# POOL instead of ACT scales the upper words of fifteen raw output weights

## The chip, the cores and the metric

The kernel runs on one core of one Trainium2 chip. The metric is the device time of one execution in microseconds (us), the median of several. A core has five engines, each with an instruction stream of its own that runs in order: TensorE (PE, whose weight loads are listed as PEld), VectorE (DVE), ScalarE (ACT), GpSimd (POOL) and SyncE (SP, which here issues all DMAs). [...]

## The reference

A windowed attention with 8 heads over 4 sequences of 768 positions, then a feed-forward block with a squared ReLU on the 3072 rows of 512 values:

```python
scores_l = scale * np.matmul(q, k.transpose(0, 1, 3, 2))          # kept where |i - j| < 16
scores_s = scale * np.einsum('bhsd,bhnd->bhsn', q, k_sum) + np.log(block)
a = softmax(concatenate([scores_l_masked, scores_s], axis=-1))
x = np.matmul(a, np.concatenate([v, v_sum], axis=2))               # to [3072, 512]
h = x @ w_in                                                       # [3072, 2048]
r = np.maximum(h, 0.0)
g = s * (r * r) + b
return (g @ w_out).astype(np.float32)
```

`k_sum` is the maximum and `v_sum` the mean over blocks of 32 positions. The weights `w_in` and `w_out` arrive as 64-bit floats.

## The kernel before

The 3072 rows are cut into 12 chunks `c` of 256 rows. For each chunk the attention is computed in four head pairs `p`, and the feed-forward block in 16 hidden blocks `f` of 128: `hidden` (PE, L403) makes the block, `activate` squares it, `project` (PE, L442) adds it to the chunk's output. Chunk 0 multiplies in plain 32-bit floats; later chunks use each operand split in a high and a low part.

The weights of a block are two tiles, ("in", f) and ("out", f), of 128x512 numbers of 64 bits. They come by DMA as they are, 512 KB each (`load_weights`, L111), into tiles named `wraw`, and are made 32-bit floats on the chip. `scale_weights` works in place on the raw words: L118 multiplies the upper word, read as a 32-bit float, by 2^-112, and L119 multiplies the lower word by 2^-29 and writes it as an integer. Both were on ACT. `convert_weights` on DVE then puts the parts together: L132 shifts the scaled upper word and masks it, L134 adds the sign bit to it, L136 adds the lower word; the result is `wf_in_f` or `wf_out_f`. From block 2 on, in and out are converted together, each of the three steps for in and then for out. Block f of chunk 0 needs `wf_in_f` in `hidden` and `wf_out_f` in `project`; in chunk 1 `split_weights` (L145 on ACT, L147 on DVE) makes the parts for later chunks.

All 32 tiles are thus converted while chunk 0 runs, from about 18 to 87 us, beside the attention of chunks 0 and 1: maximum and mask on DVE (L314), exponentials on ACT (L327), normalization on DVE (L337), copies of results on ACT (L353, L384) and the low part of the attention's output on DVE (L386). POOL builds masks in the first 8 us, then has nothing until it copies block maxima behind the window's keys (L250) for chunk 2 at 69 us. From chunk 1 on it computes `g` (L423) and fills values (L255).

The order of everything is written out by hand: the string `FIRST_ORDER` for the start (A is `scale_weights`, B `convert_weights`, H `hidden`, J `activate`, P `project`), and a plan of steps after it, one step for each hidden block. Scaling of block f stands at step f - 3 and conversion at step f - 2. Nothing is rescheduled after that, so each engine runs its instructions in the order in which the code issues them. The tiles `wraw` share 16 slots with other tiles, and SP's queue loads into a slot when its last user is done.

Of the kernel before, what the change touches and what calls it, by code (L numbers as in the profile page):

```python
# [14 lines left out]
AF = mybir.ActivationFunctionType  # L15
ALU = mybir.AluOpType
# [28 lines left out]
def windowed_attention_then_relu2_ffn(ctx, tc, qk, vwin, kt, vt, kq, vrow, wp, sb, out):  # L45


    nc = tc.nc
# [49 lines left out]
    for base, sign in ((0, 1), (BLOCK - 1, -1)):  # L98
        nc.gpsimd.affine_select(
            out=mean4[:, KR - 4 : KR], in_=mean4[:, KR - 4 : KR], compare_op=ALU.is_ge, fill=0.0,  # L100
# [12 lines left out]
    def scale_weights(key):  # L113


        raw = w_raw[key]
        top = raw[:, :, 1].bitcast(F32)
        nc.scalar.activation(top, top, AF.Copy, scale=2.0**-112)  # L118
        nc.scalar.activation(raw[:, :, 0].bitcast(I32), raw[:, :, 0], AF.Copy, scale=2.0**-29)  # L119

    def convert_weights(*keys):
# [351 lines left out]
    for n, name in enumerate(FIRST_ORDER.split()):  # L473
        kind, i = name[0], int(name[1:])
        if kind in loads:
            at(FIRST + 1, n, loads[kind], i)
        elif kind == "R":
            at(FIRST + 1, n, *((mean_of_rows, i) if i < 3 else (mean_done,)))
        elif kind == "A":
            at(FIRST + 1, n, scale_weights, ("in" if i % 2 == 0 else "out", i // 2))  # L480
        elif kind == "W":
            at(FIRST + 1, n, keep_warm, i)
        elif kind == "Z":
            at(FIRST + 1, n, scores_of_maxima, i)
        elif kind in steps:
            at(FIRST + 1, n, steps[kind], 0, i)
            ahead.add((kind, i))
        elif kind == "B":
            at(FIRST + 1, n, convert_weights, ("in" if i % 2 == 0 else "out", i // 2))
        elif kind == "D":  # L490
            at(FIRST + 1, n, convert_weights, ("in", i), ("out", i))
        elif kind in halves:
            for j in range(2):
                at(FIRST + 1, n, halves[kind], 0, i, j)
        else:
            at(FIRST + 1, n, stages[kind], 0, i)
# [42 lines left out]
    for f in range(NF):  # L539
        for side in ("in", "out"):  # L540
            if f >= 6:
                at(f - 9, LOAD, load_weights, (side, f))
            if 2 * f + (side == "out") >= FIRST_SCALED:
                at(f - 3, WEIGHTS, scale_weights, (side, f))
        if f >= FIRST_TURNED:
            at(f - 2, WEIGHTS, convert_weights, ("in", f), ("out", f))
        for side in ("in", "out"):
            at(NF - 3 + f, SPLIT, split_weights, (side, f))
# [72 lines left out]
```

## Time and profile before

| | |
|---|---|
| median of 3 runs | 641.46 us (639.6 to 641.55) |
| profiled execution, first to last instruction | 639.9 us |
| mean granted TensorE clock | 0.999 of full speed |
| ACT L118, upper words | 32 of 128x512, median 672 ns |
| ACT L119, lower words | 32 of 128x512, median 676 ns |
| DVE L132, L134, L136 for one tile | medians 418, 682 and 680 ns |
| POOL L423, 128x256 | 176, mean 623 ns |
| POOL between 8 and 64 us | no instruction |

Of the profiled execution only its span is listed; the runs' times include what lies ahead of the first instruction and behind the last. In the views, each row of a timeline gives the start and the length in us, the engine, the line, the operation and its tiles (written, then read), and in brackets how long the engine was idle before it and what released it. [...]

### The profile page before, as it was taken

Reading aid. Unit: us, or ns where it says so; the run is one execution under the profiler, and the core shown is the slowest. Engines: PE = TensorE matmul, PEld = TensorE weight load, DVE = VectorE, ACT = ScalarE, POOL = GpSimd, SP = SyncE. Lnnn points to the kernel's source line nnn. Section 1 sums busy time; section 2 is a strip of 40 time slices with the busy share of each in tenths; the row PEclk is TensorE's granted clock in tenths of the full one; section 3 lists DMA queues with packets and bytes.
Section 4 is the critical chain, followed back from the end, with each engine's and each line's share of the span. In section 5 each row is a group of like instructions: output and inputs, shape, how many; then the busy total and the mean of one; then the engine's idle time right before and its main releaser. Section 6 shows DMA issues by size and latency. Waiting matters only on the chain.

```text
span 639.9 us, 14293 instructions
## 1 busy us (share of the span) xinstructions
PE 631.2 (99%) x5316; PEld 553.3 (86%) x5316; DVE 329.4 (51%) x1081; ACT 327.7 (51%) x982; POOL 165.1 (26%) x325
## 2 busy tenths in 40 slices
PE   9899999999999999999999999999999999999997
PEld 7566678889999999999998998998999899899896
DVE  5997988885436335436526235345624514512311
ACT  3999988845437436426346345346336336423321
POOL 3000004143142421331251151151141232232211
PEclk9999999999999999999999999999999999999999
DMA  9999406035102211600700400700530400200000
GB/s 330 385 387 362 133 1 188 2 103 192 49 2 83 96 39 54 203 14 30 214 22 2 166 28 11 256 1 14 142 109 14 165 2 14 71 2 1 34 1 34
DMA packets 25606, 63.27 MB, mean 99 GB/s; under 512 B 3968, under 2 KB 3968, under 8 KB 25536
## 3 DMA queue, kind: packets, MB, share of 16 engines
q1 hardware_dynamic: 25536, 62.36, 29.1%
q8 instruction: 42, 0.69, 0.4%
q14 instruction: 28, 0.23, 0.1%
HBM read 55.90 MB, written 6.29 MB: 97 GB/s over the span
## 4 chain that ended last, share of the span: by engine, by line
PE 91%; ACT 6%; DVE 2%; issue 0%; DVEq 0%
PE po L442 40%; PE ph L403 39%; PE pav L374 3%; PE pt L346 3%; PE ps L293 3%; ACT wraw L118 2%; ACT wraw L119 2%; PE warm L202 1%; ACT pr L327 1%; ACT r L413 1%; PE pm L210 0%; PE ps L297 0%; ACT g L419 0%; ACT r L412 0%; DVE wf_in L136 0%
## 5 line engine op out<-in xcount | busy, mean ns | idle before, releaser
L423 POOL TENSOR_SCALAR g<-r,sb_col 128x256 f32<-128x256 f32 x176 | 109.5, 623 | 386.6 <-ACT r L413 282.2
L412 ACT ACTIVATE r<-ph 128x256 f32<-128x256 f32 x192 | 72.5, 378 | 214.9 <-PE ph L403 201.4
L425 DVE CAST gh<-g 128x256 fp32r<-128x256 f32 x176 | 53.3, 303 | 249.4 <-POOL g L423 241.9
L442 PE MATMUL po<-wh,gl 128*128 128x512 f32 x352 | 141.1, 401 | 0.0
L442 PE MATMUL po<-wh,gh 128*128 128x512 f32 x352 | 138.5, 393 | 0.0
L442 PE MATMUL po<-wl_out,gh 128*128 128x512 f32 x352 | 137.4, 390 | 0.0
L403 PE MATMUL ph<-xh,wl_in 128*128 128x256 f32 x704 | 110.2, 279 | 0.0
L403 PE MATMUL ph<-xl,wh 128*128 128x256 f32 x704 | 108.6, 276 | 0.0
L403 PE MATMUL ph<-xh,wh 128*128 128x256 f32 x704 | 108.6, 276 | 0.0
L403 PEld LDWEIGHTS ph<-xh,wl_in 128*128 128x128 f32 x704 | 97.2, 188 | 5.2 <-ACT r L413 0.5
L427 DVE TENSOR_TENSOR gl<-g,gh 128x256 fp32r<-128x256 f32 x176 | 81.0, 460 | 30.5 <-PE po L442 13.9
L403 PEld LDWEIGHTS ph<-xl,wh 128*128 128x128 f32 x704 | 93.4, 188 | 0.0
L403 PEld LDWEIGHTS ph<-xh,wh 128*128 128x128 f32 x704 | 92.9, 188 | 0.0
L413 ACT ACTIVATE r<-r 128x256 f32<-128x256 f32 x192 | 80.3, 418 | 6.1
L327 ACT ACTIVATE pr<-pr,mn 128x120 f32<-128x120 f32 x176 | 67.0, 382 | 32.0 <-DVE mn L314 31.9
L442 PEld LDWEIGHTS po<-wh,gh 128*128 128x128 f32 x352 | 66.1, 188 | 14.4
L442 PEld LDWEIGHTS po<-wh,gl 128*128 128x128 f32 x352 | 66.2, 188 | 13.9 <-issue 1.6
L442 PEld LDWEIGHTS po<-wl_out,gh 128*128 128x128 f32 x352 | 66.2, 188 | 13.0
L255 POOL COPY vw<-vsum 24x256 f32<-24x256 f32 x80 | 38.6, 513 | 10.6 <-PE po L442 4.5
L403 PEld LDWEIGHTS ph<-x,wf_in 128*128 128x128 f32 x128 | 23.6, 190 | 12.4 <-issue 2.9
L450 ACT COPY o<-po 128x512 f32<-128x512 f32 x24 | 14.1, 587 | 38.8 <-PE po L442 36.2
L403 PE MATMUL ph<-x,wf_in 128*128 128x256 f32 x128 | 31.1, 385 | 2.2 <-ACT pr L327 1.3
(82 smaller groups left out, 636.8 us busy)
## 6 DMA issues: line engine op xcount, KB each, us to landing
wraw<-in_wp_dram SPq DMA_DIRECT2D x32, 512.0 KB
qk<-in_qk_dram SPq DMA_DIRECT2D x44, 368.0 KB
vw<-in_vwin_dram SPq DMA_DIRECT2D x48, 192.0 KB
out_dram<-o SPq DMA_DIRECT2D x24, 256.0 KB
kraw<-in_kt_dram SPq DMA_DIRECT2D x12, 384.0 KB
vraw<-in_vt_dram SPq DMA_DIRECT2D x12, 252.0 KB
kq<-in_kq_dram SPq DMA_DIRECT2D x4, 512.0 KB
vraw<-in_vt_dram SPq DMA_DIRECT2D x6, 264.0 KB
```

Source lines behind the costliest of these rows:

```text
L255: filler(c).tensor_copy(vw_t[c, p][WIN:KR, e], vsum[bi][WIN : WIN + NB, 2 * p + e, :].unsqueeze(1).to_broadcast([NB, NSUB, D]),)
L293: nc.tensor.matmul(o, qi, kw[r, i, :], start=True, stop=True)
L327: nc.scalar.activation(pr, pr, AF.Exp, bias=mn_of[c, p][:, n : n + 1], scale=-1.0, accum_out=sm_of[c, p][:, n : n + 1])
L346: nc.tensor.transpose(pt_of[c, p][:KR, n * P : (n + 1) * P], pr[:, n, :], ident)
L374: nc.tensor.matmul(oi, vw[:, e, i, :], pi, start=True, stop=True)
L403: nc.tensor.matmul(ph, w[:, kc * P : (kc + 1) * P], x[:, kc], start=(n == 0), stop=(n == len(terms) - 1))
L412: nc.scalar.activation(r, ph, AF.Relu)
L413: nc.scalar.activation(r, r, AF.Square)
L423: nc.gpsimd.tensor_scalar(g, r, s_col, b_col, ALU.mult, ALU.add)
L425: nc.vector.tensor_copy(gh, g)
L427: nc.vector.tensor_tensor(gl, g, gh.bitcast(F32), ALU.subtract)
L442: nc.tensor.matmul(po[t], a[:, t * P : (t + 1) * P], w, start=(f == 0 and n == 0), stop=(f == NF - 1 and n == len(terms) - 1),)
```

## The change

In `scale_weights` the upper words of the output weights of blocks 1 to 15 are multiplied by POOL. The output weights of block 0, all 16 tiles of input weights, and all lower words stay on ACT.

```diff
         raw = w_raw[key]
         top = raw[:, :, 1].bitcast(F32)
-        nc.scalar.activation(top, top, AF.Copy, scale=2.0**-112)
+        if key[0] == "out" and key[1] > 0:
+            nc.gpsimd.tensor_scalar(top, top, 2.0**-112, None, ALU.mult)
+        else:
+            nc.scalar.activation(top, top, AF.Copy, scale=2.0**-112)
         nc.scalar.activation(raw[:, :, 0].bitcast(I32), raw[:, :, 0], AF.Copy, scale=2.0**-29)
```

Three lines are added, so that L119 of before is L122 after it, L132 is L135, and so on.

ACT's queue before, from the g of block 1 on (`wraw_323` and `wraw_346` are the in and out tiles of block 3, then follow those of blocks 4 and 5):

```order
L419 ACTIVATE g0_481<-r_478,sb_col_89 128x256
L118 ACTIVATE wraw_323<-wraw_323 128x512
L119 ACTIVATE wraw_323<-wraw_323 128x512
L118 ACTIVATE wraw_346<-wraw_346 128x512
L119 ACTIVATE wraw_346<-wraw_346 128x512
L118 ACTIVATE wraw_377<-wraw_377 128x512
L119 ACTIVATE wraw_377<-wraw_377 128x512
L118 ACTIVATE wraw_379<-wraw_379 128x512
L119 ACTIVATE wraw_379<-wraw_379 128x512
```

And the same place after the change:

```order
L422 ACTIVATE g0_481<-r_478,sb_col_89 128x256
L121 ACTIVATE wraw_323<-wraw_323 128x512
L122 ACTIVATE wraw_323<-wraw_323 128x512
L122 ACTIVATE wraw_346<-wraw_346 128x512
L121 ACTIVATE wraw_377<-wraw_377 128x512
L122 ACTIVATE wraw_377<-wraw_377 128x512
L122 ACTIVATE wraw_379<-wraw_379 128x512
```

One of the four ACT instructions of each block is gone; the rest keep their order. POOL's queue after the change, at the last five of the moved instructions (output weights of blocks 11 to 15), with the first fills of keys behind them:

```order
L119 TENSOR_SCALAR wraw_555<-wraw_555 128x512
L119 TENSOR_SCALAR wraw_592<-wraw_592 128x512
L119 TENSOR_SCALAR wraw_640<-wraw_640 128x512
L119 TENSOR_SCALAR wraw_681<-wraw_681 128x512
L119 TENSOR_SCALAR wraw_736<-wraw_736 128x512
L253 COPY qk_827<-ksum_164 128x4x24
L253 COPY qk_829<-ksum_190 128x4x24
```

Before, those fills came right behind the masks; now all fifteen stand between, with nothing of another kind among them. In DVE's queue nothing moves; what changes is for whom it waits. Before, at the conversion of block 3:

```order
L132 TENSOR_SCALAR wf_in_3_521<-wraw_323 128x512 [waits DMAHW3_49,Activation_49]
L132 TENSOR_SCALAR wf_out_3_522<-wraw_346 128x512 [waits DMAHW4_49,Activation_49]
L134 SCALAR_TENSOR_TENSOR wf_in_3_521<-wraw_323,wf_in_3_521 128x512 [waits DVE_49]
L134 SCALAR_TENSOR_TENSOR wf_out_3_522<-wraw_346,wf_out_3_522 128x512 [waits DVE_49]
L136 ISA wf_in_3_521<-wraw_323,wf_in_3_521 128x1024 [waits DVE_49]
L136 ISA wf_out_3_522<-wraw_346,wf_out_3_522 128x1024 [waits DVE_49,Activation_49]
```

After it:

```order
L135 TENSOR_SCALAR wf_in_3_521<-wraw_323 128x512 [waits DMAHW3_49,Activation_49]
L135 TENSOR_SCALAR wf_out_3_522<-wraw_346 128x512 [waits DMAHW4_49,Pool_49]
L137 SCALAR_TENSOR_TENSOR wf_in_3_521<-wraw_323,wf_in_3_521 128x512 [waits DVE_49]
L137 SCALAR_TENSOR_TENSOR wf_out_3_522<-wraw_346,wf_out_3_522 128x512 [waits DVE_49]
L139 ISA wf_in_3_521<-wraw_323,wf_in_3_521 128x1024 [waits DVE_49,Activation_49]
L139 ISA wf_out_3_522<-wraw_346,wf_out_3_522 128x1024 [waits DVE_49,Activation_49]
```

The first step for the out tile waits for POOL instead of ACT.

## The prediction

> **What bounds the kernel now.** The page comes first: its span, the busy shares, and the shares of the chain that ended last.
>
> ```profile
> span 639.9 us, 14293 instructions
> PE 631.2 (99%) x5316; PEld 553.3 (86%) x5316; DVE 329.4 (51%) x1081; ACT 327.7 (51%) x982; POOL 165.1 (26%) x325
> PE 91%; ACT 6%; DVE 2%; issue 0%; DVEq 0%
> ```
>
> The matrix engine PE carries 91% of the chain; ACT carries 6%, about 38 us. Averages hide where those lie, so the second view is the table of busy time by stretch:
>
> ```profile
> core 0: us, PE busy (x) PEld busy (x) DVE busy (x) ACT busy (x) POOL busy (x), PEclk, DMA share, GB/s
> 40.00:48.00 8.00, 8.00 (x59) 5.16 (x58) 7.93 (x25) 7.87 (x19) 0.00 (x0) 1.00 1.03 365
> 56.00:64.00 8.00, 8.00 (x83) 5.46 (x82) 4.71 (x12) 7.90 (x22) 0.00 (x0) 1.00 1.03 358
> ```
>
> While the first chunk runs and weights are converted (about 24 to 90 us), ACT **and** DVE are both full; POOL is empty. DVE has room in one stretch only. Third view, DVE's waits between 24 and 92 us (total, times, longest):
>
> ```profile
> DVE xl L386 <- ACT xh L384: 3.2, 1, 3.2
> DVE wf_out L132 <- ACT wraw L118: 0.5, 1, 0.5
> ```
>
> That is all DVE lost there, 3.68 us with the 3.22 and 0.46 that the timeline gives for them. So DVE is nearly as much the limit as ACT. Fourth view, the chain in order of time (start, length):
>
> ```profile
> 59.49 0.56 ACT wraw L118
> 62.24 0.42 DVE xl L386
> 69.74 0.68 DVE wf_in L136
> 70.55 1.97 PE ph L403 x8
> ```
>
> Up to 62 us the chain runs on ACT, from 62.24 to 70.4 on DVE, and from 70.55 it stays on PE until the end of the first chunk, and nearly without a break until the program ends. So what the change does to the time is what it does to the matmul that starts at 70.55 (hidden block 11): if that is late by x, the end is late by x. After it, PE waits for nothing that conversion delivers; the last block's weights are there 2.25 us ahead (85.54 + 0.68, against 88.47):
>
> ```profile
> 85.54 0.68 DVE L136 CUSTOM_DVE_ANT_0 wf_in<-wraw,wf_in 128x1024 uint16<-128x1024 uint16 x1
> 88.47 1.89 PE L403 MATMUL ph<-x,wf_in 128*128 128x256 f32 x8
> ```
>
> Where PE stood before 70.55 says how much could be won:
>
> ```profile
> 39.26 1.10 PE L403 MATMUL ph<-x,wf_in 128*128 128x256 f32 x4 [1.26 <-ACT pr L327]
> 51.69 0.70 PE L403 MATMUL ph<-x,wf_in 128*128 128x256 f32 x2 [0.27 <-ACT r L412]
> 70.55 0.67 PE L403 MATMUL ph<-x,wf_in 128*128 128x256 f32 x2 [0.47 <-DVE wf_in L136]
> 38.44 0.68 DVE L136 CUSTOM_DVE_ANT_0 wf_in<-wraw,wf_in 128x1024 uint16<-128x1024 uint16 x1
> ```
>
> The first wait is put down to ACT, but the weights of that block came from DVE at 38.44 + 0.68 = 39.12: it is DVE's. Of the three, counted from the usual spacing of such groups, some 1.3, 0.4 and 0.6 us are lost.
>
> **The change part by part.** *Removed from ACT:* 15 of these 32 instructions, at the chain's step of 0.57 us (0.67 each, the next starting earlier):
>
> ```profile
> L118 ACT ACTIVATE wraw<-wraw x32: 650/672/710, 18.1 to 79.6; 128x512 f32<-128x512 f32 x32
> ```
>
> 15 × 0.57 = 8.6 us of ACT time. Little of it can reach the end: DVE does all of its work still. DVE's 3.68 us of idle time can go, no more. And PE can at best be earlier by 0.46 at block 4 (DVE's wait at 33 us), 0.4 at block 7 (ACT's) and 0.6 at block 11: 1.5 us is the ceiling.
>
> *Added to POOL:* 15 TENSOR_SCALARs of 128x512, in POOL's queue ahead of the first fill of window keys (L250). Each waits for its DMA, not for ACT's turn, so it runs when its weights land. The last loads go out in this row (SP's queue) and ACT scales the last one 24 us later, from data that had long landed:
>
> ```profile
> 51.92 3.82 SPq L111 DMA_DIRECT2D wraw<-in_wp_dram  x4
> 79.62 0.68 ACT L118 ACTIVATE wraw<-wraw 128x512 f32<-128x512 f32 x1
> ```
>
> So all 15 run between about 20 and 66 us, several us ahead of need. POOL's own length is thus hidden: even at 1.5 us each, with one due every 3 to 4 us, nothing waits for it. The fills of keys behind them started at 69.25 and come after the last of the 15 in any case.
>
> *What is not hidden is the memory port.* POOL and DVE get in each other's way here. The timeline, POOL alone, then with DVE:
>
> ```profile
> 95.31 0.56 POOL L423 TENSOR_SCALAR g<-r,sb_col 128x256 f32<-128x256 f32 x1 [24.18 <-ACT r L413]
> 504.98 0.59 POOL L423 TENSOR_SCALAR g<-r,sb_col 128x256 f32<-128x256 f32 x1 [0.17 <-POOL g L423]
> 505.25 0.60 DVE L427 TENSOR_TENSOR gl<-g,gh 128x256 fp32r<-128x256 f32 x1
> 506.15 0.43 DVE L427 TENSOR_TENSOR gl<-g,gh 128x256 fp32r<-128x256 f32 x1
> ```
>
> The subtraction takes 0.43 alone and 0.60 when POOL began 0.27 earlier: it was held until 0.27 + 0.17 = 0.44 after POOL's start. The same, the other way round, among the very conversions at issue:
>
> ```profile
> 133.41 0.26 POOL L250 COPY qk<-ksum 128x96 f32<-128x96 f32 x1 [0.56 <-issue]
> 324.29 0.40 POOL L255 COPY vw<-vsum 24x256 f32<-24x256 f32 x1 [0.44 <-PE po L442]
> 69.06 0.68 DVE L134 SCALAR_TENSOR_TENSOR wf_out<-wraw,wf_out 128x512 uint32<-128x512 uint32 x1
> 69.25 0.61 POOL L250 COPY qk<-ksum 128x96 f32<-128x96 f32 x1 [61.58 <-DVE wf_in L134]
> 69.66 0.75 DVE L136 CUSTOM_DVE_ANT_0 wf_in<-wraw,wf_in 128x1024 uint16<-128x1024 uint16 x1
> ```
>
> A copy that takes 0.26 alone (0.40 at 256 elements) takes 0.61 under L134: it waits for the running DVE instruction, then gets in before the next one, which takes 0.75 instead of 0.68. So **POOL's wait is free, but each POOL operation pushes DVE back** by what it streams.
>
> How much? The copy pushed DVE by 0.07, so 0.19 of its 0.26 lies off the port. Taking 0.19 from L423's 0.56 leaves 0.37 for 256 elements, thus 0.74 for 512. From the two copies, (0.40 − 0.26) / 160 = 0.88 ns an element, thus 0.45 for 512. The new instruction is L423's kind with one operation and no operand from memory instead of two with: between these ends I take 0.60. Below zero it cannot go; at zero lies the case that POOL never gets in between.
>
> How often? DVE's groups between 24 and 64 us:
>
> ```profile
> L134 DVE SCALAR_TENSOR_TENSOR wf_out<-wraw,wf_out 128x512 uint32<-128x512 uint32 x10 | 6.8, 683 | 0.1
> L136 DVE CUSTOM_DVE_ANT_0 wf_out<-wraw,wf_out 128x1024 uint16<-128x1024 uint16 x10 | 6.8, 682 | 0.3
> L132 DVE TENSOR_SCALAR wf_out<-wraw 128x512 uint32<-128x512 uint32 x10 | 4.2, 420 | 0.5 <-ACT wraw L118 0.5
> L314 DVE CUSTOM_DVE_ANT_0 pr<-ps,mask_mid 128x120 f32<-128x120 f32 x12 | 2.6, 274 | 0.0
> ```
>
> With their twins for wf_in, the conversions keep DVE for about 10 × 2 × (0.60 + 0.60 + 0.34) = 30.8 of 40 us at the steps of the timeline, 77%; what reads PSUM (L314) or one small operand leaves the port free. I take three hits in four. L132 never meets POOL before the change; it runs at twice the element rate of the others (512 elements in a step of 0.34), and L425, a cast that does so too (0.28 alone), was lengthened beside POOL's L255:
>
> ```profile
> 104.89 1.16 POOL L255 COPY vw<-vsum 24x256 f32<-24x256 f32 x2
> 105.30 0.49 DVE L425 CAST gh<-g 128x256 fp32r<-128x256 f32 x1
> 505.77 0.28 DVE L425 CAST gh<-g 128x256 fp32r<-128x256 f32 x1
> ```
>
> So I count L132 as one that collides; were it free, the share would be 60% and the sum below 1.5 us less.
>
> **Sum.** DVE is pushed back by 15 × 0.60 × 0.75 = 6.75 us before block 11, and gets back at most its 3.68 us of idle time (with DVE late, neither wait is left). Block 11, for which PE already waits on DVE, is late by 6.75 − 3.68 = **3.1 us**, and the end with it. The lost 0.6 us at 70.55 is no reserve, since DVE sets that time before and after. At 0.45 the sum is 5.1 − 3.7 = +1.4; at 0.74 it is 8.3 − 3.7 = +4.6. The profiled execution has a span of 639.9 us; the median of the runs is 641.46, the 1.6 us between lying around the span or in the spread (639.6 to 641.55). Counting from the median: 641.46 + 3.1 = **644.5 us**.
>
> [...]
>
> **The rivals.**
> *B, cheap stream:* the one-operation form streams like the copy, 0.45 or less. For it: its simpler work. Against: the instruction's kind. 641.46 + 1.4 = 642.9.
> *C, DVE keeps the port; not slower:* POOL slips in only where DVE pauses. One row of before is for it:
>
> ```profile
> 108.76 0.42 DVE L427 TENSOR_TENSOR gl<-g,gh 128x256 fp32r<-128x256 f32 x1
> 108.96 1.18 POOL L423 TENSOR_SCALAR g<-r,sb_col 128x256 f32<-128x256 f32 x1
> 109.10 0.68 DVE L147 TENSOR_TENSOR wl_in<-wf_in,wh 128x512 fp32r<-128x512 f32 x1
> ```
>
> There POOL queued during one DVE instruction and the next still went first, unhurt. The row at 69.25 speaks against it. It decides from where the push is under 3.68 / (15 × 0.75) = 0.33 us; in full it gives the ceiling, 641.46 − 1.5 = 640.0. That the relief of ACT simply buys nothing lies between this and B.
> *D, lock for the whole instruction:* alone, the new instruction takes 0.19 + 0.74 = 0.93; a push of 0.88 gives 15 × 0.88 × 0.75 − 3.7 = +6.2, 647.7. The 0.44 of 0.59 speaks against it.
>
> **How the numbers follow.** Forecast 0.47, B 0.24, C 0.17, D 0.12. The range reaches from C's better part to D's lower part, 640.7 to 647.2. A measurement of this kernel can tell about 0.3% (1.9 us) from no change: slower means over 643.4, faster under 639.5. Forecast's case is slower but for its low end (0.43), D is slower (0.12), B has a little of it (0.05): 0.60. C reaches faster with its tail only: 0.06. The rest is 0.34.
>
> **What would show it.** In the changed profile ACT should have idle time between 24 and 64 us, DVE should have next to none there (the 3.2 us wait for xh gone), and L132, L134 and L136 that follow a POOL operation should be longer than 0.42 and 0.68 by about 0.6. POOL's 15 operations should lie between 20 and 66 us, alone some 0.6 to 0.9 us, and longer where DVE runs. Block 11 should start at about 73.6. I am wrong if DVE's conversions keep their lengths (C), if POOL's operations run later than 66 us and DVE waits for them, or if PE after block 11 waits again for DVE, so that the loss grows beyond the sum.

## The result, and the profile after

| | before | after |
|---|---|---|
| median of 5 runs each, side by side | 639.66 us (639.32 to 641.55) | 643.73 us (641.24 to 644.59) |
| ratio | | 1.0053, 95% interval 1.0037 to 1.0068 |
| span of the profiled execution | 639.9 us | 639.5 us (its run took 641.24 us) |

The change makes the kernel slower by about 0.53%, 3.4 us (2.4 to 4.3); the two medians lie 4.1 us apart. Three single executions far from the rest (1273 us, and 650.7 and 650.9 us at a granted clock of 0.95) are left out of all ratios here. The two profiled spans don't show it: the profile of before comes from the upper end of its runs, that of after from the lower end. The start differs by chance (last section), so the two are compared from block 0's first `hidden` matmul on, at 24.52 us before and 21.98 us after.

The page of after, the same three lines as before (the third is the chain):

```profile
span 639.5 us, 14325 instructions
PE 627.7 (98%) x5316; PEld 550.4 (86%) x5316; DVE 335.7 (52%) x1081; ACT 320.4 (50%) x967; POOL 192.5 (30%) x340
PE 94%; DMA 2%; DVE 2%; ACT 1%; issue 0%; POOL 0%; DVEq 0%
```

ACT lost 15 instructions and 7.3 us; DVE has the same 1081 instructions and 6.3 us more. The busy time by stretch, same columns as before:

```profile
40.00:48.00 8.00, 7.28 (x55) 4.18 (x53) 7.93 (x21) 6.34 (x19) 5.08 (x3) 1.00 1.03 366
56.00:64.00 8.00, 8.00 (x76) 5.19 (x76) 7.93 (x17) 7.38 (x17) 4.79 (x3) 1.00 1.04 362
```

DVE is full in both (7.93; in the second it had 4.71 before), ACT is not any more, and PE stood for 0.72 us in the first. The chain's 2% of DMA is not the cause: in the lists of waits between 24 and 72 us, loads hold up ACT once, by 0.6 us, and PE and DVE not at all. The waits between 24 and 92 us (PE) and 24 and 72 us (ACT); DVE has none at all:

```profile
PE ph L406 <- DVE wf_in L139: 3.1, 4, 2.2
PE po L445 <- DVE g L420: 0.7, 1, 0.7
PE ph L406 <- ACT r L416: 0.7, 1, 0.7
```

```profile
ACT pr L330 <- DVE mn L317: 3.5, 3, 1.6
ACT r L415 <- PE ph L406: 0.8, 2, 0.5
```

What ACT won it spends waiting for DVE's maxima. Now the timeline of POOL, DVE and PE at two places:

```profile
30.94 0.42 DVE L135 TENSOR_SCALAR wf_out<-wraw 128x512 uint32<-128x512 uint32 x1
31.07 1.75 POOL L119 TENSOR_SCALAR wraw<-wraw 128x512 f32<-128x512 f32 x1 [0.59 <-DVE wf_in L135]
31.27 1.14 DVE L137 SCALAR_TENSOR_TENSOR wf_in<-wraw,wf_in 128x512 uint32<-128x512 uint32 x1
32.34 0.68 DVE L137 SCALAR_TENSOR_TENSOR wf_out<-wraw,wf_out 128x512 uint32<-128x512 uint32 x1
...
37.16 1.61 POOL L119 TENSOR_SCALAR wraw<-wraw 128x512 f32<-128x512 f32 x1 [1.28 <-DMA wraw<-in_wp_dram]
37.27 1.12 DVE L139 CUSTOM_DVE_ANT_0 wf_in<-wraw,wf_in 128x1024 uint16<-128x1024 uint16 x1
...
38.54 1.75 PE L406 MATMUL ph<-x,wf_in 128*128 128x256 f32 x7 [2.15 <-DVE wf_in L139]
```

POOL's instruction starts while a DVE instruction runs; the next DVE instruction takes 1.14 instead of 0.68 us, the one after it 0.68 again. At 37.27 the same happens to the weights of block 4, and PE, done with block 3, stands 2.15 us for them (at the same place before, 1.26). All POOL instructions of this kind (least, median and most, ns, then first and last start):

```profile
L119 POOL TENSOR_SCALAR wraw<-wraw x15: 1609/1812/2240, 22.4 to 66.9; 128x512 f32<-128x512 f32 x15
```

Beside each of the fifteen, one DVE instruction (beside one of them two) is longer than the median of its kind before. Eleven are longer by 0.44 to 0.49 us, the rest by 0.13 to 0.36; with one of 0.06 at 69 us, 6.29 us between 16 and 94 us. This sum is called **the pushes** below; it is 0.07 us in the profile of before. The instruction pushed is the next that DVE starts in eleven of the fifteen; in the other four it is one that comes behind instructions reading the matrix engine's output memory (PSUM: L317, L389). Those keep their length beside POOL: up to 94 us L317 takes 0.27 to 0.28 us in 12 cases beside a POOL instruction and in 27 without one, L389 0.41 in the one case beside and 0.41 to 0.42 without. ACT's instructions, summed in the same way, are longer by 0.10 us (0.05 before): POOL slows DVE and not ACT. The chain in order of time (start, length, what):

```profile
43.77 0.27 DVE pr L317
...
44.07 1.62 ACT pr L330 x8
45.70 0.57 ACT wraw L121
46.27 1.14 ACT wraw L122 x2
47.41 0.27 ACT r L415
...
47.70 0.43 ACT r L416
...
48.17 1.97 PE ph L406 x8
```

Here is a second way in which a late DVE can reach PE: the maxima are late, the exponentials behind them too, and what stands behind those in ACT's queue (scaling, then an `r`) with them; PE gets block 6 going at 48.17. The chain names one releaser only. The weights of block 6, pushed as well, come at the same moment:

```profile
46.90 1.12 DVE L139 CUSTOM_DVE_ANT_0 wf_in<-wraw,wf_in 128x1024 uint16<-128x1024 uint16 x1
```

Around here PE starts some 0.14 us behind weights that it waits for (block 4: 37.27 + 1.12 = 38.39, start 38.54; block 11 before: 69.74 + 0.68 = 70.42, start 70.55). Block 6's are ready at 46.90 + 1.12 = 48.02 and PE starts at 48.17, so both ways end together there. From there the chain is on PE to the end of the chunk, and no wait of PE for DVE is listed again. At block 11 the weights are there 0.15 us before PE starts:

```profile
69.27 0.74 DVE L139 CUSTOM_DVE_ANT_0 wf_in<-wraw,wf_in 128x1024 uint16<-128x1024 uint16 x1
...
70.16 1.97 PE L406 MATMUL ph<-x,wf_in 128*128 128x256 f32 x8
```

That is the same handover, so PE has no slack: from the start of `project` before it to this matmul it takes 70.16 − 68.39 = 1.77 us, where one block earlier it takes 1.72. DVE and PE come to block 11 together, and DVE is the later by about 0.05 us.

From block 0's first matmul to block 11's: 70.55 − 24.52 = 46.03 us before, 70.16 − 21.98 = 48.18 after.

### The profile page after: what moved, and what is told of

It is laid out like the page before. It is cut to its first block, busy times and chain, and to the rows that moved or that the text cites. A ratio compares the mean times of both kernels' runs of the same rounds, so it can differ in the third digit from the quotient of the medians.

```text
span 639.5 us, 14325 instructions
## 1 busy us (share of the span) xinstructions
PE 627.7 (98%) x5316; PEld 550.4 (86%) x5316; DVE 335.7 (52%) x1081; ACT 320.4 (50%) x967; POOL 192.5 (30%) x340
## 3 DMA queue, kind: packets, MB, share of 16 engines
HBM read 55.90 MB, written 6.29 MB: 97 GB/s over the span
## 4 chain that ended last, share of the span: by engine, by line
PE 94%; DMA 2%; DVE 2%; ACT 1%; issue 0%; POOL 0%; DVEq 0%
PE po L445 42%; PE ph L406 41%; PE pav L377 4%; PE pt L349 3%; PE ps L296 3%; DMA wraw<-in_wp_dram 1%; DMA kq<-in_kq_dram 1%; PE pm L213 1%; DVE pr L317 0%; PE pav L374 0%; ACT wraw L122 0%; POOL wraw L119 0%; PE pav L375 0%; PE ps L300 0%; DVE wf_in L137 0%
## 5 line engine op out<-in xcount | busy, mean ns | idle before, releaser
L119 POOL TENSOR_SCALAR wraw<-wraw 128x512 f32<-128x512 f32 x15 | 28.3, 1887 | 32.8 <-DMA wraw<-in_wp_dram 25.7
```

Source lines behind the costliest of these rows:

```text
L119: nc.gpsimd.tensor_scalar(top, top, 2.0**-112, None, ALU.mult)
```

## The experiments

Two theories stood at the start. **P**: each POOL instruction pushes DVE back, by 0.44 to 0.49 us in eleven of the fifteen cases above, and that is the loss. **Q**: not the pushes but the new order of work costs, in which ACT runs ahead and then stalls in its queue. Unless a diff says otherwise, an experiment starts from the changed kernel. Where the prediction and the expectations speak of a port, what the runs show is the pushing; what POOL and DVE hold each other up at is not shown. All profiles in one table: the stretch is that from block 0's first matmul to block 11's, and "rest" is the span (given to 0.1 us) less block 11's start.

| kernel | pushes, us | block 0, us | block 11, us | stretch, us | rest, us | ratio to before, 95% interval |
|---|---|---|---|---|---|---|
| before | 0.07 | 24.52 | 70.55 | 46.03 | 569.35 | 1 |
| before, again | 0.08 | 22.14 | 67.86 | 45.72 | 569.34 | 1.0000, 0.9987 to 1.0012 |
| nobody scales | 0.14 | 21.74 | 65.81 | 44.07 | 569.29 | 0.9974, 0.9962 to 0.9986 |
| half length | 2.77 | 22.56 | 68.95 | 46.39 | 569.25 | 1.0006, 0.9995 to 1.0016 |
| POOL besides ACT | 5.82 | 22.81 | 73.66 | 50.85 | 569.34 | 1.0062, 1.0048 to 1.0076 |
| after | 6.29 | 21.98 | 70.16 | 48.18 | 569.34 | 1.0053, 1.0037 to 1.0068 |
| after, again | 7.58 | 23.07 | 71.93 | 48.86 | 569.37 | 1.0054, 1.0036 to 1.0072 |
| two operations, again | 5.18 | 22.10 | 69.38 | 47.28 | 569.32 | 1.0032, 1.0019 to 1.0045 |
| after, g on ACT | 7.80 | 24.54 | 73.76 | 49.22 | 569.34 | 1.0032, 1.0016 to 1.0048 |
| nobody scales, g on ACT | 0.13 | 21.76 | 65.59 | 43.83 | 569.31 | 0.9969, 0.9957 to 0.9981 |
| two operations, g on ACT | 5.90 | 22.26 | 69.35 | 47.09 | 569.25 | 1.0043, 1.0027 to 1.0058 |
| POOL for blocks 4 to 10 | 2.61 | 21.99 | 68.72 | 46.73 | 569.28 | 1.0015, 1.0001 to 1.0030 |
| probe | 5.68 | 22.65 | 71.30 | 48.65 | 569.30 | one run, 642.3 us |

**Before, again** (no edit): what two runs of one kernel differ by.

> The kernel before, unchanged, for its spread and a second trace. Both theories: ratio 1.000. The profile of before began block 0 of chunk 0 (its first matmul) at 24.52 us, that of after at 21.98, though their instructions up to there are the same. If this is a matter of the run and not of the change, runs of this kernel fall into two groups about 2 us apart (near 639.5 and 641.5), and in either group the stretch from the first matmul of block 0 to that of block 11 stays at 46.0 us, against 48.2 in the profile of after.

Median 639.7 us. The stretch agrees within 0.31 us; the start, with no change at all, within 2.4. The two groups of runs are there: eight at 638.9 to 640.0 us, two at 641.4 and 641.5.

**Nobody scales.** The upper words of the fifteen tiles are multiplied by no engine; DVE masks one bit more in the step that it does anyway. That gives the same weights where they are below 2 in size.

```diff
         if key[0] == "out" and key[1] > 0:
-            nc.gpsimd.tensor_scalar(top, top, 2.0**-112, None, ALU.mult)
+            pass
...
+            keep = 0x3FFFFFFF if key[0] == "out" and key[1] > 0 else 0x7FFFFFFF
+            nc.vector.tensor_scalar(w, top, 3, keep, ALU.logical_shift_left, ALU.bitwise_and)
```

> Leaves out the multiplication of the fifteen upper words altogether (and clears one exponent bit in DVE's mask so that the numbers stay finite; same instruction). ACT is relieved as in the change, POOL does nothing. Theory P (POOL's use of the port pushes DVE back by 0.46 us each): no lengthened DVE instructions, the stretch from block 0 to block 11 falls to about 44.5 us, and the time is about 1.5 us under before, ratio 0.998. Rival Q (the new order of waits costs: with ACT ahead, its queue now stalls on DVE's minima and holds up the squares that PE waits for): the stretch stays near 48 us and the ratio near 1.004.

Median 637.6 us, faster than before by 0.26%, as P expected. ACT is relieved and runs in the changed kernel's order, POOL does nothing, and the loss turns into a gain. Q falls as the cause of the loss: the order is the same here.

**Half length.** POOL multiplies 256 of the 512 columns, with the mask of the run above:

```diff
-            nc.gpsimd.tensor_scalar(top, top, 2.0**-112, None, ALU.mult)
+            nc.gpsimd.tensor_scalar(top[:, 0:256], top[:, 0:256], 2.0**-112, None, ALU.mult)
```

> POOL multiplies 256 of the 512 upper words of each of the fifteen tiles; the other half is left out (mask as in the run without the POOL operation). Theory P with the push being what is streamed: each push falls from 0.46 to about 0.23 us, their sum from 6.2 to 3.1, the stretch from block 0 to block 11 is about 45.5 us, ratio 0.999 to 1.000. If the push is the lock for a whole instruction with a large fixed part (0.3 us or more), the sum stays over 4.5 us and the stretch over 46.5. Rival Q: unchanged from after, near 48 us.

Median 639.88 us. The timeline, where L140 is L139 of after:

```profile
37.64 1.09 POOL L119 TENSOR_SCALAR wraw<-wraw 128x256 f32<-128x256 f32 x1 [2.19 <-DMA wraw<-in_wp_dram]
37.89 0.90 DVE L140 CUSTOM_DVE_ANT_0 wf_out<-wraw,wf_out 128x1024 uint16<-128x1024 uint16 x1
```

Half the elements, half the push: 0.22 us. The loss against "nobody scales" falls from 0.79% to 0.32%. The pushes (2.77 us) are what P expected, the stretch (46.39) is longer than its 45.5; the part on the prediction comes back to that.

**POOL besides ACT.** ACT scales all 32 tiles as before, and POOL multiplies the fifteen by 1.0 ahead of it:

```diff
         if key[0] == "out" and key[1] > 0:
-            nc.gpsimd.tensor_scalar(top, top, 2.0**-112, None, ALU.mult)
-        else:
-            nc.scalar.activation(top, top, AF.Copy, scale=2.0**-112)
+            nc.gpsimd.tensor_scalar(top, top, 1.0, None, ALU.mult)
+        nc.scalar.activation(top, top, AF.Copy, scale=2.0**-112)
```

> The kernel before, with the fifteen POOL operations added: POOL multiplies the same upper words by 1 in place when they land, then ACT scales them as before. ACT is not relieved. Theory P: DVE is pushed back by about 6 us in all; up to 3.7 us of it fall into its idle time, but ACT, no faster than before, ends that idle time no earlier; the stretch from block 0 to block 11 grows by 2 to 4 us, ratio 1.003 to 1.006. Rival Q, under which POOL's operations are harmless and ACT's lead is what costs: ratio 1.000.

Median 643.51 us: before, with nothing taken away, is made slower by 0.62%, a little more than P's 1.003 to 1.006, and the stretch grows by 5 us instead of 2 to 4. Not all of that is pushes. ACT now waits for POOL, by ACT's waits from 24 to 72 us:

```profile
ACT wraw L120 <- POOL wraw L119: 3.4, 2, 1.7
```

So this run bounds the pushes' share from above and no more.

**After, again, and the g of chunk 0 on ACT.** Six of chunk 0's sixteen g are DVE's. Moving them to ACT, which the change gave room, relieves DVE by 0.4 us each (0.33 from start to start):

```diff
-    G_BY_DVE = (0, 2, 8, 9, 12, 13)
+    G_BY_DVE = ()
```

> The changed kernel once more, for its spread and a second trace. Theory P: fifteen pushes of about 0.45 us on DVE again, 5.5 to 6.5 us in sum whatever the start of the run, the stretch from block 0 to block 11 at 48 to 49.5 us, ratio 1.004 to 1.007. If the first trace was an accident of how POOL's operations fell, sum and stretch differ from it by more than 1.5 us.

> The changed kernel, with the six g of chunk 0 that DVE computes given to ACT: 6 x 0.33 = 2.0 us less for DVE, 6 x 0.5 = 3 us more for ACT. Theory P (DVE is now the limit, ACT waits 7.5 us for PE's results): 1 to 2 us less than the changed kernel, ratio to the kernel before 1.001 to 1.003. Rival Q (ACT's queue is what holds up PE): no better than the changed kernel, ratio 1.005 or more.

> As the run without the POOL operation (the multiplication of the fifteen upper words left out), with the six g of chunk 0 on ACT besides. PE's waits in that run come to about 1.1 us between 20 and 92 us, so under theory P no more than that is left: 0 to 1 us under it, ratio to the kernel before 0.996 to 0.9975.

The changed kernel repeats (643.5 us), but its pushes, 7.58 us, are more than the 5.5 to 6.5 expected. With the g moved it takes 641.71 (1.0032, between what P and Q expected), and "nobody scales" takes 637.46 with them and 637.6 without, the fastest kernel here but not told apart from its neighbour. All these intervals overlap with their partners'. The profile of "after, again" shows why the sum is larger, a push that comes twice under one POOL instruction:

```profile
48.38 1.84 POOL L119 TENSOR_SCALAR wraw<-wraw 128x512 f32<-128x512 f32 x1 [1.67 <-DMA wraw<-in_wp_dram]
48.71 1.12 DVE L139 CUSTOM_DVE_ANT_0 wf_out<-wraw,wf_out 128x1024 uint16<-128x1024 uint16 x1
49.76 0.75 DVE L135 TENSOR_SCALAR wf_in<-wraw 128x512 uint32<-128x512 uint32 x1
```

L139 is longer by 0.44 us and L135, next, by 0.33. Five of that profile's pushes are such second ones. DVE also stands for POOL once there, for 0.4 us.

**Two operations.** The same product, followed by adding zero in the same instruction:

```diff
-            nc.gpsimd.tensor_scalar(top, top, 2.0**-112, None, ALU.mult)
+            nc.gpsimd.tensor_scalar(top, top, 2.0**-112, 0.0, ALU.mult, ALU.add)
```

> The changed kernel, with POOL's instruction given a second operation (add 0.0), so that it is of the kind of the g instruction that the prediction scaled its 0.74 us from. If what an element costs on the port depends on the number of operations: pushes near 0.74 us, 9 to 11 us in sum, the stretch from block 0 to block 11 at 51 to 53 us, ratio about 1.011. If one element takes 0.88 ns whatever is done with it, as in POOL's copies: pushes stay at 0.45 us, sum about 6.2, ratio as for the changed kernel, and the prediction erred by charging the longer start of the g instruction to the port.

> The changed kernel once more with the two-operation form of POOL's multiplication (times 2^-112, plus 0.0), since the earlier look at it has a profile with a clock of 0.949, which its parts after block 11 can't be read from. Theory P (each POOL instruction pushes DVE by what it streams): the form of the instruction changes POOL's own length, not the stream. POOL's instructions 0.65 to 1.2 us instead of 1.6 to 2.2, the push on DVE summed over 16 to 94 us 4.5 to 6.0 us (the changed kernel: 6.3 to 7.8), block 0's first matmul to block 11's 46.5 to 48.0 us, ratio to before 1.002 to 1.005. Rival L (the long POOL instruction is what costs: DVE waits for the scaled words): with POOL twice as fast the loss would be gone, ratio 0.998 to 1.000, stretch 44.0 to 45.7 us.

The first took 641.92 us (ratio 1.0035, 1.0023 to 1.0047), the second 641.01 (1.0032). The profile of the second:

```profile
L119 POOL TENSOR_SCALAR wraw<-wraw x15: 657/987/2078, 22.5 to 68.5; 128x512 f32<-128x512 f32 x15
```

```profile
31.57 0.98 POOL L119 TENSOR_SCALAR wraw<-wraw 128x512 f32<-128x512 f32 x1 [0.59 <-DVE wf_out L135]
31.95 1.13 DVE L137 SCALAR_TENSOR_TENSOR wf_out<-wraw,wf_out 128x512 uint32<-128x512 uint32 x1
```

POOL's instruction is a little over half as long, and still a push is 0.45 us. There are no second pushes, two of the fifteen push nothing, and some 0.2% of time goes (by two pairs of runs whose intervals overlap). Rival L, that POOL's own length is what costs, fell: the loss stays at 0.32%, inside what P said, and so do the pushes (5.18) and the stretch (47.28). One of the two that push nothing is a case of its own:

```profile
28.90 2.08 POOL L119 TENSOR_SCALAR wraw<-wraw 128x512 f32<-128x512 f32 x1 [2.74 <-DMA wraw<-in_wp_dram]
31.01 0.43 DVE L135 TENSOR_SCALAR wf_out<-wraw 128x512 uint32<-128x512 uint32 x1 [0.57 <-POOL wraw L119]
```

DVE's three instructions between (L139 twice, L135) keep their 0.68, 0.68 and 0.41 us: here POOL did not get in between them, as rival C had it, and DVE then stood 0.57 us for POOL's result. That cost is not in the pushes.

**Two operations, with the g on ACT,** and then the same **with POOL for blocks 4 to 10 alone**:

```diff
-        if key[0] == "out" and key[1] > 0:
+        if key[0] == "out" and 4 <= key[1] <= 10:
```

> The two-operation form, and the six g of chunk 0 that DVE makes go to ACT, which the change gave room. Each takes about 0.4 us from DVE, 2.4 us in all, of which the earlier pair of runs (changed kernel 1.0054, with g on ACT 1.0032) showed about 1.4 us at the end. Theory P: the push stays (4.5 to 6.0 us summed), DVE is relieved: ratio 1.000 to 1.002. Rival L: 0.995 to 0.998.

> As the run before it, but POOL scales the upper words of the output weights of blocks 4 to 10 alone (7 instead of 15); the other 8 are ACT's again. Theory P: half the pushes (2.2 to 3.0 us summed, 0.22 to 0.25 us at the end for each), ratio 0.998 to 1.0005, between the run before it and the one where nobody scales them (0.9969). If ACT's time were what matters in place of DVE's, the eight instructions given back would cost 8 x 0.57 = 4.6 us of ACT time and the ratio would be above that of the run before it, 1.003 or more.

The first misses what P expected: 641.99 us, 1.0043, no better than without the g moved (1.0032), and the intervals overlap. DVE has less to do, but the chain goes through ACT (its profile is of its fastest run, 640.34 us, and does not show where the slower ones lost their time):

```profile
52.33 0.27 DVE pr L317
...
52.64 0.64 ACT pr L330 x3
...
53.32 0.95 ACT pr L330 x5
54.27 0.57 ACT wraw L121
54.84 1.13 ACT wraw L122 x2
55.97 0.27 ACT r L415
...
56.31 1.97 PE ph L406 x8
```

Work given to ACT stands in its queue among the exponentials that PE's next block hangs on. But the weights of that block come at the same time, lengthened by a push (55.02 + 1.14 = 56.16, 0.15 us before the matmul), so that ACT's queue sets this start is not shown:

```profile
55.02 1.14 DVE L139 CUSTOM_DVE_ANT_0 wf_in<-wraw,wf_in 128x1024 uint16<-128x1024 uint16 x1
```

Whether moving the g helps at all is left open. The second run, with 7 POOL instructions, has half the pushes (2.61 us, as P said), but 1.0015 lies above P's range and below the rival's 1.003. Nine of its twelve runs lie at 639.5 to 640.1 us and three at 643.0 to 643.3; its profile is of one of the nine. In that profile DVE waits for ACT again:

```profile
DVE wf_out L135 <- ACT wraw L121: 1.1, 2, 0.7
```

With eight scalings back on ACT, ACT is part of the limit, as it was before the change. It does not tell the two apart.

**Probe.** Six POOL instructions more, on a tile of zeros behind the masks, for the length by itself:

```diff
+    for n in (512, 256):
+        nc.gpsimd.tensor_scalar(zeros[:, :n], zeros[:, :n], 2.0, None, ALU.mult)
+        nc.gpsimd.tensor_scalar(zeros[:, :n], zeros[:, :n], 2.0, 0.0, ALU.mult, ALU.add)
+        nc.gpsimd.tensor_copy(zeros[:, :n], zeros[:, :n])
```

> The disputed length by itself: six POOL operations more, in place on a 96x512 tile of zeros right behind the masks, at 5 to 12 us, where DVE reads little: the one-operation TENSOR_SCALAR, the two-operation one and a copy, at 512 elements and then at 256. Their results are not used. If the one-operation form is slow by itself (theory F): 1.3 to 1.6 us at 512 elements, against about 0.65 for the two-operation one and 0.6 for the copy; at 256 about 0.7 to 0.9, 0.45 to 0.55 and 0.4. If it was long in the changed kernel only because it waits for DVE (theory W): all three within 0.2 us of each other, 0.5 to 0.9 us at 512. The time of the run itself is expected within 0.5% of the two-operation form's.

POOL's timeline (L223 has one operation, L224 two, L225 is the copy):

```profile
6.54 1.49 POOL L223 TENSOR_SCALAR vsum<-vsum 96x512 f32<-96x512 f32 x1
...
8.81 0.61 POOL L224 TENSOR_SCALAR vsum<-vsum 96x512 f32<-96x512 f32 x1
...
9.51 0.61 POOL L225 COPY vsum<-vsum 96x512 f32<-96x512 f32 x1
10.20 0.84 POOL L223 TENSOR_SCALAR vsum<-vsum 96x256 f32<-96x256 f32 x1
11.13 0.40 POOL L224 TENSOR_SCALAR vsum<-vsum 96x256 f32<-96x256 f32 x1
11.60 0.39 POOL L225 COPY vsum<-vsum 96x256 f32<-96x256 f32 x1
```

The form with one operation is slow by itself (theory F), (1.49 − 0.84) / 256 = 2.5 ns an element against 0.82 with two and 0.86 for the copy. W, that it only waits for DVE, falls. (A reduction on DVE runs beside the first 0.41 us of the first row; at 256 elements, where only short DVE instructions that read PSUM run beside, the one-operation form is twice as long all the same, 0.84 us against 0.40.)

## Why the prediction was right, and where not

The time forecast was 644.5 us, the measured median 643.73; the increase forecast was 3.1 us, the measured one 3.4 (2.4 to 4.3). Direction and mechanism held; that the number came so close is in part luck (steps 4, 5 and 8). By its steps:

1. *The end follows block 11.* Held, and more sharply than it was argued: in thirteen profiles of eleven different kernels the span less block 11's start is 569.25 to 569.37 us. Whatever any of these edits did, it did before that matmul. The matmul itself, forecast for about 73.6 us, started at 70.16 because the program began earlier; with the start of the first profile it would be 24.52 + 48.18 = 72.7.
2. *The ceiling of a gain, 1.5 us.* Held within the spread: "nobody scales" is that case, with DVE spared every push, and gains 0.26%, 1.7 us.
3. *POOL's own length is hidden.* Nearly held, though the length (0.6 to 0.9 us alone, "even at 1.5") was wrong: 1.6 to 2.2 us, and 1.49 alone at 96 partitions. DVE never waits for POOL in the profile of after, and once, for 0.4 us, in that of "after, again".
4. *The push of 0.60 us.* Mis-sized. It is 0.44 to 0.49, half of that at half the elements. Of the two ends of the bound it is the copies' rate, 512 × 0.88 ns = 0.45, to which rival B had held; the choice between the ends went by the wrong row, the longer instruction. What that row takes beyond a copy of as many elements (0.56 against 0.40 us at 256) was charged to the push; with two operations, the kind of that row, a push of 512 elements is 0.45 us too.
5. *Three hits in four.* Mis-sized the other way: all fifteen push, eleven in full. The arrival is not random: eleven times in fifteen POOL comes in behind the running DVE instruction, and the four times that DVE goes on with instructions that read PSUM, it pushes a later one. That those are not pushed themselves held (L317, 0.27 to 0.28 us beside POOL as without it). Small operands, counted as free, stay as they are in before (L335, 0.18 us in 16 cases beside POOL and in 32 without), but one is pushed in the profile of after (L337, 0.13 us at 61.31). The two misses nearly cancel, which is luck: 15 × 0.60 × 0.75 = 6.75 us forecast, 6.29 and 7.58 in the two profiles.
6. *Less DVE's 3.68 us of idle time.* Held for DVE, only in part for PE. From the moment that block 0's input weights are converted to the same moment of block 11, DVE takes 49.2 and 49.3 us in the two profiles of before. After the change it takes 2.3 and 3.9 us more, where the pushes less 3.68 give 2.6 and 3.9; with two operations 1.3 more (1.5), at half length 0.6 less (0.9 less), with "nobody scales" 4.0 less (3.5 less). PE's stretch, 45.88 us in the mean of before's two, grows by 2.3 and 3.0 after the change and by 1.4 with two operations. But "nobody scales" wins only 1.8 of DVE's 4.0, as PE gets to block 11 2.1 us after its weights. At half length even the sign turns: DVE is 0.6 us early at block 11, and the stretch grows by 0.5. Of before's idle time on DVE, 3.2 us lie after 59 us, too late to help block 8. Its weights come 2.3 us later than before (counted the same way), PE starts it 0.15 us behind them, and from there it runs to block 11 without a break.
7. *DVE sets block 11.* Held, but by 0.05 us, and not in the way that it was argued: PE stands no 0.6 us there any more. Its waits have moved ahead. Up to block 11 they come to 4.5 us after the change and 2.6 before: 1.5 against 0.6 by block 2, 2.15 against 1.26 at block 4, 0.9 against nothing at blocks 5 and 6, and nothing against 0.7 behind that. So the end is late by the sum because DVE and PE come to block 11 together, which was not foreseen. ACT's queue as a second way from DVE to PE was not in the working either; whether it cost anything by itself stays open, as the weights of block 6 are late as well.
8. *The base.* The median of 641.46 was of three runs, two of them from the late end; with five it is 639.66. So the forecast time is close partly because a base 1.8 us too high met an increase too low by 1.0 (3.1 against the 4.1 between the medians).

Of the rivals, C (DVE keeps the port) fell with fifteen pushes of fifteen; what it says happens to single instructions only, one with two operations and one at half length. D (held for the whole instruction, a push of 0.88 us) fell with pushes of 0.46 us under instructions of 1.6 to 2.2; none in the profile of after is over 0.49. B's price was right for a single push, though not for its reason (simpler work: two operations push as much), and its sum (+1.4 us) was not, since it kept the three in four.

## What to carry to other kernels

Here the work moved to an idle POOL was paid by DVE, which was full (7.93 of 8 us): fifteen instructions pushed it by 6.29 and 7.58 us in the two profiles. For another kernel that gives a first estimate, to be measured there: count every POOL instruction as one hit of its elements times a copy's rate (0.88 ns here) and set the sum against DVE's idle time in that stretch, not against what the relieved engine wins. Here the count is 15 × 0.45 = 6.75 us, and the seven profiles of the table with fifteen instructions of full size show pushes of 5.18 to 7.80. The measured pushes less the idle time told how late DVE was, to within 0.5 us. Whether the end was as late depended on where the idle time lies and on which block PE waits for, so do the sum for each such block and not for the whole stretch alone. The better move was not another engine but none: one more bit in a mask that DVE applies anyway did away with the instruction, for weights below 2 in size, and beat both kernels (637.6 us). And a median of three can lie at the edge of a kernel's spread; compare stretches inside the profiles, from the same event to the same event.

## What the hardware showed that was not expected

POOL's multiplication with one operation and no second takes 1.49 us for 96x512 by itself, and with a useless second operation 0.61. Why is not settled, nor why the long form still pushes DVE by 0.45 us, or why it sometimes pushes twice. What decides when POOL gets in is open too: in the profile of after it is in eleven cases of fifteen at the next DVE instruction, but once with two operations (28.90 us) and once at half length (28.91 us) DVE ran three more at their usual length before it stood for POOL, 0.6 and 0.8 us.

The start of the program varies by over 2 us with no change. Two profiles of the kernel before, PE's timeline, first before, then before again:

```profile
5.68 2.50 PE L202 MATMUL warm<-ones 128*128 128x128 f32 x8
...
11.58 3.20 PE L210 MATMUL pm<-vn,mean 128*120 128x512 f32 x4
```

```profile
5.14 1.48 PE L202 MATMUL warm<-ones 128*128 128x128 f32 x8
...
9.81 1.95 PE L210 MATMUL pm<-vn,mean 128*120 128x512 f32 x4 [0.41 <-DMA vn<-in_vrow_dram]
```

The same matmuls take 1.6 to 1.7 times as long, though from 5 to 12 us and from 12 to 20 us both profiles show a granted clock of 1.00, and block 0 starts at 24.52 instead of 22.14. What makes them longer is not shown.
